# Two value projections by a seven-product block scheme, in a two-layer attention and gated-MLP kernel on one core

## The chip, the core and the metric

The kernel runs on one core of a Trainium2 chip. The metric is the device time of one execution in microseconds; of the kernel before there are three runs, 1532.43, 1533.35 and 1533.71 us, with the median 1533.35. The profile is that of one further execution (1532.7 us, of which 1531.0 us lie between the first and the last instruction). TensorE's granted clock was 1.000 of full speed in it.

Engines are named as in the profile: PE is TensorE's matmul (PEld its weight loads), DVE is VectorE, ACT is ScalarE, POOL is GpSimd, SP is the engine that issues most DMA transfers. "L836" is line 836 of the kernel before.

## The reference, cut to what matters

```python
def _A_ref(x, wqkv, wo):          # B=1, S=2048, D=1024, H=32 heads of Dh=32
    qkv = (x @ wqkv).reshape(B, S, 3, H, Dh).transpose(2, 0, 3, 1, 4)
    q, k, v = qkv[0], qkv[1], qkv[2]
    # each position attends to W=8 positions, 2 apart, backwards
    logits = einsum("bhsd,bhswd->bhsw", q, kg) * Dh ** -0.5   # masked at the start
    attn = softmax(logits)
    o = einsum("bhsw,bhswd->bhsd", attn, vg)
    return o.transpose(0, 2, 1, 3).reshape(B, S, D) @ wo

def _B_ref(x, w1, w3, w2):        # F=3584
    return (silu(x @ w1) * (x @ w3)) @ w2

x = x + _A_ref(layernorm(x), wqkv, wo)      # layer 0, the same weights
x = x + _B_ref(layernorm(x), w1, w3, w2)
x = x + _A_ref(layernorm(x), wqkv, wo)      # layer 1
x = x + _B_ref(layernorm(x), w1, w3, w2)
```

The change concerns the last third of `x @ wqkv`, the values v: a product of a chunk of 512 positions (1024 x 512) with a 1024 x 1024 weight, in layer 1 only.

## The kernel before

The 2048 positions are cut into four chunks of 512. A unit is a layer and a chunk; the eight units' MLP stages follow each other on TensorE, u = 0 to 7. After the MLP stages 1 to 4 come the products q, k and v of the unit three further on, that is of layer 1's chunks 0 to 3. The attention itself runs on VectorE beside the next MLP stages, and its output tiles (matmul with `wo`, "po") are pushed in between MLP groups.

```python
    for u, (l, c) in enumerate(units):
        ...
        q = u + 3
        with_q = 1 <= u and q < len(units)
        b_stage(u, with_q)                       # MLP of the unit
        if with_q:
            for which in range(3):               # q, k, v of unit u + 3
                if which == 2:
                    between(False, True)
                q_part(*units[q], which, [weight("qkv"), weight("qkv")])
                release(2)
```

A part q, k or v is computed plainly: for each of eight output tiles eight matmuls of 128 x 512, a cast out of PSUM by ScalarE (L840), and a store of every two tiles.

```python
    def q_part(l, c, which, ws, then=()):
        ...
            for t in range(t0, t0 + SG):
                ps = bank("ps")
                for kk in range(KT):                                   # KT = 8
                    nc.tensor.matmul(ps[:], lhsT=ws[kk // KH][:, kk % KH, t::KT], rhs=xnT[:, kk, :],
                                     start=(kk == 0), stop=(kk == KT - 1))        # L836
                nc.scalar.copy(sgt[:, t - t0, :], ps[:])                          # L840
            nc.sync.dma_start(qkv_d[l][which][:, t0:t0 + SG, c * CH:(c + 1) * CH], sgt)
```

The MLP stages from u = 2 on compute `x @ w1` and `x @ w3` by a scheme of Strassen's kind: the operands are cut into 2 x 2 blocks, and seven block products (P1 to P7) of sums of blocks stand for eight. The sums of the weights' blocks are made once, stored to device memory (`t_d`) and loaded again for each group as two tiles, "early" (for P1, P5, P6, P2) and "late" (P7, P3, P4). The sums of the activations' blocks are made by VectorE (`norm_sums`, L298; one of them, for P7, overwrites a block of xnT). One product is eight matmuls of 128 x 256.

```python
    def pipeline(key, groups, consume, done, last, fill=None):
        sides = dict(P1=(0, xnT[:, 0:KQ, 0:HT]), P5=(1, sums[:, 0]), P6=(2, sums[:, 1]), P2=(3, xnT[:, KQ:KT, 0:HT]),
                     P7=(0, xnT[:, 0:KQ, HT:CH]), P3=(1, sums[:, 2]), P4=(2, xnT[:, KQ:KT, HT:CH]))
        ...
        def head_part(i, name):
            if name == "P1":
                G["A"] = acc()
                r = run(G, name, G["A"], True)
                G["B"] = acc()
                nc.scalar.copy(G["B"][:], G["A"][:])                 # L1064: P6 and P2 wait for it
            elif name == "P5":
                G["D"] = acc()
                r = run(G, name, G["D"], True)
                nc.scalar.activation(s5, G["D"][:], ACTF.Copy, ...)  # L1069
            elif name == "P6":
                r = run(G, name, G["A"], False, G["tB"])             # adds onto A
                nc.scalar.copy(su, G["A"][:])                        # L1073: P7 waits for it
                nc.vector.tensor_tensor(G["D"][:], G["D"][:], su, op=ALU.add)   # L1076: P3 waits
            elif name == "P2":
                r = run(G, name, G["B"], False, G["tB"])
                consume(G, 0, G["B"][:], r)
            elif name == "P7":
                r = run(G, name, G["A"], False, G["tU"])
                nc.vector.scalar_tensor_tensor(s22, G["A"][:], G["inv"], s5, ...)   # L1088: P4 waits
                consume(G, 3, s22, G["tC"])
            elif name == "P3":
                r = run(G, name, G["D"], False, G["tD"])
                consume(G, 1, G["D"][:], r)
            else:                                                    # P4
                r = run(G, name, G["A"], False, G["tC"])
                consume(G, 2, G["A"][:], r)

        for i in range(n + 1):      # the tail of group i-1 lies between the products of group i
            for name, tail in (("P1", "P7"), ("P5", "P3"), ("P6", "P4"), ("P2", None)):
                if i < n:
                    head_part(i, name)
                if tail and i:
                    head_part(i - 1, tail)
                    if fill and i == n and tail != "P4":
                        fill(int(tail == "P3"))      # in the MLP: first products with w2
```

Before a weight's sums are made its size is measured (squares on ScalarE with an accumulator, one small matmul with ones, a few small VectorE operations) for a power of two that scales it into FP16. Each weight is loaded into one of six tiles; a tile's `release` lets the next load in the fixed sequence start. Background work is placed by the kernel's own estimate of the engines' clocks when it is built: the order within each engine is fixed. Such background work on ScalarE are the normalizations of coming stages (two passes per row block for the moments, L318, and one to apply them, L345), and the exponential of the softmax (L629), which needs another function table than the MLP's Silu.

## Time and profile before

| | before |
|---|---|
| time, median of 3 | 1533.35 us |
| span of the profiled run | 1531.0 us |
| PE busy | 1518.1 us |
| DVE busy | 1201.8 us |
| ACT busy | 884.1 us |
| "ps" matmuls of 128 x 512 (q, k, v; L836) | 1469 recorded, 320.4 us |
| "st" matmuls of 128 x 256 (seven products; L1052) | 4704, 32% of the chain |
| moved by DMA | 439.56 MB, mean 287 GB/s |

A row of the groups gives a line, engine, operation, output and inputs, shape and count, then busy time, the mean of one in ns, and the idle time of the engine ahead of it with what ended it. A matmul's own duration [...] is longer than its distance from the next; the distance is read from the timeline, from start to start. A row of the timeline is a start, a duration, the engine, the line, the operation, and in brackets the idle time ahead with its releaser. The four stages of q, k and v in layer 1 lie at 514.3 to 556.3, 700.7 to 742.6, 885.0 to 926.9 and 1072.7 to 1114.1 us.

### The profile page before, as it was taken

The numbers are of one execution on the slowest core, as the hardware profiler recorded it, in microseconds if no ns is written. First come the engines' busy times: TensorE is split into PE (matmuls) and PEld (weight loads), VectorE is DVE, ScalarE is ACT, GpSimd is POOL, SyncE is SP. The second block draws the span as 40 slices with busy tenths as digits, with TensorE's granted clock in tenths as the row PEclk, the third lists the DMA queues.
The fourth block names the chain that finished last, engine by engine and source line by source line (L and its number), as shares of the span: only waits on it lengthen the run. The fifth ranks groups of instructions, "written<-read, shape, count | busy, mean of one in ns | idle before, by whom it ended". The sixth has DMA issues, their size and how long they took to land.

```text
span 1531.0 us, 25095 instructions
## 1 busy us (share of the span) xinstructions
PE 1518.1 (99%) x9594; PEld 989.5 (65%) x9634; DVE 1201.8 (78%) x2126; ACT 884.1 (58%) x1388; POOL 153.7 (10%) x308
## 2 busy tenths in 40 slices
PE   9999999999999999999999999999999999999999
PEld 7666644444444577575786767766677767686865
DVE  4688998889989898989698958898678986435445
ACT  3885476567665357455565564756557445554643
POOL 1210102121211101001011010100111000000000
PEclk9999999999999999999999999999999999999999
DMA  9777969798997888979779997898969988878885
GB/s 321 202 218 215 253 226 330 272 304 289 306 320 247 280 316 294 347 264 303 263 269 324 346 268 282 280 323 302 323 225 333 338 296 282 306 272 334 318 294 203
DMA packets 261432, 439.56 MB, mean 287 GB/s; under 512 B 73856, under 2 KB 201088, under 8 KB 245056
## 3 DMA queue, kind: packets, MB, share of 16 engines
q1 hardware_dynamic: 248464, 390.90, 76.8%
q0 software_dynamic: 12704, 46.93, 8.6%
q8 instruction: 75, 1.23, 0.3%
q14 instruction: 45, 0.37, 0.1%
q10 hardware_dynamic: 144, 0.13, 0.0%
HBM read 345.90 MB, written 67.90 MB: 270 GB/s over the span
## 4 chain that ended last, share of the span: by engine, by line
PE 97%; ACT 1%; issue 1%; DVE 0%; DMA 0%; SPq 0%; ACTq 0%
PE st L1052 32%; PE ps L836 21%; PE w L1165 16%; PE po L771 7%; PE pg L1279 6%; PE pu L1288 6%; PE acc L1310 6%; PE pq L444 1%; PE L L604 0%; DMA wqkv<-in_A_wqkv_dram 0%; ACT L629 0%; ACT L1227 0%; ACT E L629 0%; ACT sg L1227 0%; DVE x_sb L1150 0%
## 5 line engine op out<-in xcount | busy, mean ns | idle before, releaser
L836 PE MATMUL ps<-xnT,wqkv 128*128 128x512 f16 (+1 forms) x1469 | 320.4, 379 | 0.2
L1052 PEld LDWEIGHTS <-early 128*128 128x128 f16 x2688 | 262.6, 98 | 40.4 <-issue 3.5
L836 PEld LDWEIGHTS <-wqkv 128*128 128x128 bf16 x1472 | 210.6, 144 | 108.1 <-issue 2.2
L1165 PE MATMUL w<-t,hT 128*128 128x512 f16 x1008 | 226.0, 379 | 0.6 <-ACT big L1185 0.5
L1052 PEld LDWEIGHTS <-late 128*128 128x128 f16 x2016 | 197.2, 98 | 30.6 <-issue 2.5
L590 DVE TENSOR_TENSOR tree<-qT,kT 128x2048 bf16<-128x2048 bf16 x128 | 156.3, 1221 | 35.8 <-DMA kT<-qkv_d 18.2
L1052 PE MATMUL st<-xnT,late 128*128 128x256 f16 x1344 | 174.2, 273 | 2.2 <-ACT big L1073 2.2
L510 DVE TENSOR_TENSOR tree<-tree 128x1024 bf16<-128x1024 bf16 x256 | 175.6, 686 | 0.9
L1052 PE MATMUL st<-big,early 128*128 128x256 f16 x1344 | 172.3, 273 | 1.6 <-ACT sg L1227 1.1
L1165 PEld LDWEIGHTS <-hT 128*128 128x128 f16 x1008 | 98.2, 98 | 112.9 <-DVE hT L1136 2.0
L1052 PE MATMUL st<-xnT,early 128*128 128x256 f16 x1344 | 165.7, 273 | 0.0
L665 DVE TENSOR_TENSOR tree<-At,vT 128x2048 bf16<-128x2048 bf16 x128 | 156.2, 1221 | 11.9 <-DMA At<-E 10.7
L1064 ACT COPY st<-st 128x512 f32<-128x512 f32 x84 | 48.3, 575 | 128.1 <-PE st L1052 127.4
L771 PE MATMUL po<-wo,oT 128*128 128x512 bf16 x486 | 110.8, 379 | 1.3
L840 ACT CAST hT<-ps 128x512 bf16<-128x512 f32 x96 | 55.8, 585 | 90.6 <-PE ps L836 88.3
L1288 PE MATMUL pu<-xnT,w3t 128*128 128x512 f16 x448 | 105.8, 379 | 0.0
L1279 PE MATMUL pg<-xnT,w1t 128*128 128x512 f16 x448 | 105.8, 379 | 0.0
L1310 PE MATMUL acc<-w2t,hT 128*128 128x512 bf16 x437 | 97.8, 379 | 0.6
L1076 DVE TENSOR_TENSOR st<-st,big 128x512 f32<-128x512 f32 x84 | 58.4, 695 | 46.9 <-ACT big L1073 46.8
L1227 ACT ACTIVATE sg<-st,down_scale 128x512 bf16<-128x512 f32 x126 | 86.6, 687 | 11.6 <-PE st L1052 11.0
L1052 PE MATMUL st<-big,late 128*128 128x256 f16 x672 | 87.1, 273 | 0.0
L771 PEld LDWEIGHTS <-oT 128*128 128x128 bf16 x512 | 50.1, 98 | 55.7
(167 smaller groups left out, 1916.6 us busy)
## 6 DMA issues: line engine op xcount, KB each, us to landing
early<-t_d SPq DMA_DIRECT2D x84, 1024.0 KB, 6.9
late<-t_d SPq DMA_DIRECT2D x84, 768.0 KB, 6.2
t<-t_d SPq DMA_DIRECT2D x42, 1024.0 KB, 7.3
t<-t_d SPq DMA_DIRECT2D x42, 768.0 KB, 5.3
wqkv<-in_A_wqkv_dram SPq DMA_DIRECT2D x28, 1024.0 KB, 8.1
w1t<-in_B_w_dram SPq DMA_DIRECT2D x14, 1024.0 KB, 7.6
w3t<-in_B_w_dram SPq DMA_DIRECT2D x14, 1024.0 KB, 11.0
t_d<-big POOLq DMA_DIRECT2D x28, 512.0 KB, 6.2
```

What stands on the lines that cost most here:

```text
L510: nc.vector.tensor_tensor(b, b, buf[:, 4:8, :], op=ALU.add)
L590: V.tensor_tensor(pr, qT[:], kT[:, :, k0:k0 + TCH], op=ALU.mult)
L665: V.tensor_tensor(tm.rearrange("p w (a e) -> p w a e", a=4), At[:].rearrange("p a w e -> p w a e"), win, op=ALU.mult)
L771: nc.tensor.matmul(ps[:], lhsT=oT[:, t, j * P:(j + 1) * P], rhs=wo[:, t, hh * 512:(hh + 1) * 512], start=(t == 0), stop=(t == KT - 1))
L836: nc.tensor.matmul(ps[:], lhsT=ws[kk // KH][:, kk % KH, t::KT], rhs=xnT[:, kk, :], start=(kk == 0), stop=(kk == KT - 1))
L1052: nc.tensor.matmul(out[:, a, :], lhsT=w[:, a, blk, k, :], rhs=rhs[:, k, :], start=start and a == 0 and k == 0, stop=k == KQ - 1, skip_grou ...
L1076: nc.vector.tensor_tensor(G["D"][:], G["D"][:], su, op=ALU.add)
L1165: nc.tensor.matmul(out[:], lhsT=lhs[:, k, j * P:(j + 1) * P], rhs=w[:, k, :], start=start and k == 0, stop=k == nq - 1, skip_group_check=True)
L1227: nc.scalar.activation(sg[:], src, ACTF.Silu, scale=inv)
L1279: nc.tensor.matmul(pg[:], lhsT=w1t[:, kk, fi * P:(fi + 1) * P], rhs=xnT[:, kk, :], start=(kk == 0), stop=(kk == KT - 1))
L1288: nc.tensor.matmul(pu[:], lhsT=w3t[:, kk, fi * P:(fi + 1) * P], rhs=xnT[:, kk, :], start=(kk == 0), stop=(kk == KT - 1))
L1310: nc.tensor.matmul(acc[:], lhsT=hT[:, f, j * P:(j + 1) * P], rhs=tiles[hh][f // nq][:, f % nq, :], start=(f == 0), stop=(f == f1 - f0 - 1))
```

## The change

The v part of layer 1's chunks 2 and 3 goes through the seven-product pipeline in place of the plain products. For that, v's weights are measured during the plain v part of layer 1's chunk 0, their block sums are made during chunk 1 (where v is therefore computed first, so that the weight tiles can stay for the sums while q and k follow), stored to device memory and loaded as "early" and "late" tiles in chunks 2 and 3. It is meant to save TensorE one block product in eight. The casts out of PSUM with the scale taken back are ScalarE's in place of the plain casts; one of four blocks comes from VectorE. The sums of the activations' blocks are made for these two chunks as for the MLP.

The core of the diff, with cuts:

```diff
+    size_v = const.tile([P, 8], FP32, name="size_v")
+    down_v = const.tile([P, 1], FP32, name="down_v")
+    up_v = const.tile([P, 1], FP32, name="up_v")
+    blocks += [hT[:, 9:16, :].bitcast(FP16).rearrange("p b (k c) -> p b k c", k=KT // 2)]
+    t_d += [[dram.tile([P, 14, KT // 2, P], FP16, name=f"t_dv_{g}") for g in range(2)]]
...
-            seq += [("qkv", which, h) for which in range(3) for h in range(2)]
+            seq += [("qkv", which, h) for which in ((0, 1, 2), (2, 0, 1), (0, 1))[min(u, 3) - 1] for h in range(2)]
+            if u > 2:
+                seq += [("early", 2, 0), ("early", 2, 1), ("late", 2, 0), ("late", 2, 1)]
...
     def queue_q(q):
         queue_norm(key, units[q][1], range(R))
+        if q > NCH + 1:
+            adds.append([sum_later(key), None])
...
+    def size_of_v(i, w, at):
+        for k in range(KH):
+            yield 1.10, at, lambda: nc.scalar.activation(junk[:, 0:D], w[:, k], ACTF.Square,
+                                                         accum_out=size_v[:, KH * i + k:KH * i + k + 1])
+        if i == 1:
+            total_scale(size_v, up_v, down_v, got_v)
+
+    def sums_of_v(ws, at):
+        ...
+        for g in range(2):
+            for a in range(2):
+                ...
+                for i, (kh, fh) in ((0, (0, 0)), (1, (0, 1)), (3, (1, 0)), (5, (1, 1))):
+                    t = 4 * g + 2 * fh + a
+                    yield 0.65, ..., lambda: nc.scalar.activation(
+                        b[:, i], ws[kh][:, :, t::KT], ACTF.Copy, scale=up_v[:])
+                makes.append([differences(2, g, a, now["act"] + 0.1, slot), None])
...
+    def v_products(l, c):
+        def consume(G, q, src, r):
+            pair, t0 = q % 2, HT * (q // 2)
+            to = stage(G, pair)
+            if q != 3:
+                nc.scalar.activation(to[:, :, t0:t0 + HT], src, ACTF.Copy, scale=down_v[:])
+            ...                      # store when both halves of a pair are there
+        for g in range(2):
+            G = dict(m=2, g=g, inv=down_v[:])
+            G["corner"] = lambda G=G: stage(G, 1)[:, :, HT:CH]
+            groups.append(G)
+        pipeline(key, groups, consume, lambda i: between(False, i == 0), True)    # no fill
+        xnT_free[key] = now["pe"]
...
-            for which in range(3):
-                if which == 2:
-                    between(False, True)
-                q_part(*units[q], which, [weight("qkv"), weight("qkv")])
+            if u == 1:                                   # layer 1, chunk 0
+                ...                                      # q, k, v plain; size_of_v queued in v
+            if u == 2:                                   # layer 1, chunk 1
+                for which in (2, 0, 1):
+                    ...                                  # v, q, k plain; sums_of_v queued in v,
+                    ...                                  # finished after q, then 4 tiles released
+                force(makes, lambda: not any(pending))
+                continue
+            for which in range(2):                       # chunks 2 and 3
+                q_part(*units[q], which, [weight("qkv"), weight("qkv")], (), 1)
                 release(2)
+            v_products(*units[q])
```

## The prediction

> **What bounds the kernel now.** I read the busy shares first, then the chain of waits, then the waits of TensorE alone, and last the timeline at the seams that the change touches. From the page, busy time by engine and the chain that ended last:
>
> ```profile
> PE 1518.1 (99%) x9594; PEld 989.5 (65%) x9634; DVE 1201.8 (78%) x2126; ACT 884.1 (58%) x1388; POOL 153.7 (10%) x308
> ...
> PE 97%; ACT 1%; issue 1%; DVE 0%; DMA 0%; SPq 0%; ACTq 0%
> ```
>
> TensorE is busy for 1518 of 1531 us, and 97% of the chain runs over it. So a matmul taken away is worth its full duration, and a wait put into TensorE's queue costs its full length; no other engine has to be made faster for its own sake. The waits of TensorE, longest first, show how little else there is:
>
> ```profile
> PE st L1052 <- ACT big L1073: 2.2, 1, 2.2
> ...
> PE st L1052 <- ACT sg L1227: 1.1, 1, 1.1
> PE w L1165 <- ACT big L1185: 0.5, 1, 0.5
> PE st L1052 <- ACT st L1064: 0.4, 1, 0.4
> ```
>
> All four lie in layer 1 or the MLP stages before it (in the timeline at 989.8, 669.1, 1066.0 and 1234.1 us), and the chain leads from each to the same thing: the softmax's exponential (E, L629) with its table load stands in ScalarE's queue ahead of a copy that TensorE needs. They depend on where the exponential happens to fall.
>
> TensorE's timeline around layer 1's second chunk (q, k and v are 192 plain products, "ps"; "st" is the seven-product scheme of the MLP):
>
> ```profile
> 700.70 31.24 PE L836 MATMUL ps<-xnT,wqkv 128*128 128x512 f16 x144
> 731.87 0.40 PE L604 MATMUL L<-psm,gather 128*32 128x512 bf16 x4
> 732.20 10.58 PE L836 MATMUL ps<-xnT,wqkv 128*128 128x512 f16 x48
> 742.62 1.04 PE L1052 MATMUL st<-xnT,early 128*128 128x256 f16 x8
> 743.50 1.91 PE L1052 MATMUL st<-big,early 128*128 128x256 f16 x16
> ```
>
> From start to start 144 matmuls take 31.17 us, 0.2165 us each. Eight "st" matmuls, one of the seven products, take 0.873 us from start to start (MLP groups of the same window: 594.44, 595.32, 596.19).
>
> The seam itself, all engines:
>
> ```profile
> 742.82 0.59 ACT L840 CAST hT<-ps 128x512 bf16<-128x512 f32 x1 [1.14 <-PE ps L836]
> 743.50 1.91 PE L1052 MATMUL st<-big,early 128*128 128x256 f16 x16
> 743.75 0.57 ACT L1064 COPY st<-st 128x512 f32<-128x512 f32 x1 [0.34 <-PE st L1052]
> ```
>
> Product P1 runs from 742.62, P5 from 743.50, and P6 adds onto P1's accumulator, so it waits until ScalarE has copied that (L1064). The copy ends at 744.32 and P6's place is 742.62 + 2 x 0.873 = 744.37. The reader should see that the slack is 0.05 us: **anything that stands in ScalarE's queue between the last cast and this copy is a TensorE wait.**
>
> [...] 873/8 is 109.1. So halving the width is nearly free, and seven eighths of the work is seven eighths of the time. [...] 592 without and 711 ns with a scale (L1283, L910), table loads 1283. [...] the mean DMA share in the four q/k/v stages is 0.99, 0.90, 0.91 and 1.04.
>
> **The change part by part.**
>
> *Removed and added on TensorE.* One v part is 64 x 0.2165 = 13.86 us. The new one is 2 groups x 7 products x 0.873 = 12.22 us. Two parts: **-3.28 us**. One small matmul adds up the sizes; such float32 ones have 0.19 us of weight load and 0.21 busy: **+0.15**.
>
> *Head of the new v part, twice.* In the changed program's order ScalarE's queue has, after k's last cast, a normalization (L345 of before, mean 1241 ns), then P1's copy. From the end of k: cast at 0.25, normalization at 0.73 (a cast frees the queue after 0.48, as 703.11 - 702.62 shows), copy 1.97 to 2.54, so P6 starts at 2.59 and not at 1.75: 0.84 us. The second normalization stands ahead of the next copy, but P2 and P1 of the second group lie between, so it should cost nothing. **+1.7.**
>
> *Tail of the new v part, twice.* In the MLP the last three products P7, P3, P4 are interleaved with products of w2; here with nothing. P4 waits for VectorE's sum after P7 (L1088, 748 ns). In VectorE's order attention steps precede that sum: in chunk 2 three (1.14 + 0.34 + 0.61 us without their overlap) stand between P6's sum and P7's. Counting from the end of k: P6's sum of the second group ends at 10.2, these steps at 12.25, P7's sum at 13.0, while P3 ends at 12.2: 0.85. In chunk 3 only two short ones stand there: 0.15. **+1.0.**
>
> *Sizes in chunk 0.* Eight squares of 128x1024 on ScalarE between the casts of v. The trace has the same pair: cast at 713.0, square (L318) 713.47, accumulator read 714.43, next cast 714.71, which is 1.72 us for a product group of 1.73. So it just keeps pace; but the eighth square stands between the last cast and P1's copy of the MLP stage that follows: 0.25 + 0.48 + 1.24 + 0.57, the same 2.54 as above. **+0.85.**
>
> *Sums in chunk 1.* 16 scaled copies (711 ns, 11.4 us of ScalarE) and 16 differences (422 ns, 6.8 us of VectorE) during 27.7 us of v and q, where ScalarE was busy 7.3 of 13.8 and 9.8 of 13.9 us and VectorE full. Two copies and a cast are about 1.9 us against TensorE's 1.73, and six PSUM banks take up the lag. On the path: nothing. But k now comes last, the gather of the next scores stands 8 products (1.73 us) before the seam, and E before the last cast: gather at -2.06, its maximum and difference done near -0.2 (the steps follow at +0.45, +1.18 and end at +1.9), then E, cast, copy. With the table loaded in time nothing is lost, else up to 1.0: **+0.5.**
>
> *What moves.* Later scores shift by up to a stage. The places of E at 979, 1063 and 1228 us, which cost 2.19, 0.47 and 0.41, are gone: they fall in plain products or between w2's copies. One lands within an MLP group of the seventh stage, like that at 669.1 (1.1), one among w2's first products (0.5, my judgement): -3.07 + 1.6 = **-1.5.** The one at 669.1 keeps its neighbours.
>
> *Transfers.* v's weights for a chunk are 3.5 MB for 2 MB, twice, and 3.5 MB are written once. **+0.25**, a judgement: some waits, mostly hidden.
>
> Sum: -3.28 + 0.15 + 1.7 + 1.0 + 0.85 + 0.5 - 1.5 + 0.25 = -0.33 us, so 1533.35 becomes 1533.0. The gain of the eighth product is about eaten by the seams.
>
> **Rivals.** (1) *The clean gain.* The seams cost little, since P6's wait is really only part of what I count or ScalarE gets to the copies earlier: 1530 to 1531. For it: no MLP start in this trace shows a wait. Against it: there the copy has no normalization or square ahead of it. (2) *DMA becomes the bound.* With a share of 0.9 to 1.04 in these stages another 1.5 MB in each of two, and 3.5 MB of stores in chunk 1, at the stage's 270 to 340 GB/s are about 5 and 11 us of transfers; v's and q's weights are also held together in chunk 1, so four loads for the next MLP stage start only with k. If the loads come late, TensorE waits for "early" or "late": 1536 to 1540. For it: the shares. Against it: 13.9 us of k cover those four loads of 3.75 MB (11 us at 340 GB/s), the chunk-3 stage ran at 1.04 without one DMA wait on TensorE, and the new weights are loaded a stage ahead. (3) *Attention comes late.* k last delays the scores of chunk 1 by a part (14 us), and VectorE gets 26 more instructions; if an output tile is then wanted before its values are done, TensorE waits several us. Against it: the output tiles moved back by a group or more in the order too, and VectorE's slices in the last fifth are only 4 to 6 tenths busy. 1535 to 1538.
>
> **Range and chances.** The seams are worked out to perhaps 1.5 us together, the shift of the exponentials to 2, the rivals pull up more than down. 8 in 10: 1529.5 to 1536.5. Two per cent is 30.7 us, ten times anything above: faster 0.003, same 0.99, slower 0.007.
>
> **What would show it.** In the profile after: 128 fewer "ps" matmuls and 224 more "st"; two v parts of about 13.9 and 13.2 us from first P1 to the MLP's P1, each with a wait near 0.84 on the copy of P1 and one on the corner sum; a wait of 0.85 at the start of the MLP stage after layer 1's first chunk; no 2.2 us wait near 989 us. It would be wrong if TensorE waits for a DMA or for oT, if the waits at the v parts are nil (rival 1), or if new waits on E of over 2 us stand elsewhere.

## The result and the profile after

The changed kernel takes 1538.74 us (median of 4 runs, 1538.36 to 1540.13), the kernel before 1532.89 us (4 runs, 1531.49 to 1533.71): a ratio of 1.0041, 95% interval 1.0023 to 1.0058. That is 5.85 us more, where 0.3 us less was predicted, and 2.2 us above the predicted range.

The profiled run spans 1536.7 us, for 1531.0. From the page after, busy time by engine and the chain that ended last:

```profile
PE 1519.5 (99%) x9732; PEld 993.5 (65%) x9732; DVE 1219.0 (79%) x2163; ACT 915.2 (60%) x1428; POOL 158.2 (10%) x316
PE 90%; DVE 5%; DMA 2%; ACT 1%; issue 1%; POOL 0%; SPq 0%; ACTq 0%; DVEq 0%
```

PE is busy 1.4 us *longer* although it has fewer columns to multiply. The chain that ran 97% over PE now runs 5% over DVE and 2% over DMA. ACT has 31.1 us more, of which the prediction had accounted for some 10 us of squares and 11 us of copies; the copies alone take 19.4, as shown below. The waits of PE in the whole kernel after (engine, line, what it waited for; then us in total, times, longest):

```profile
PE st L1092 <- ACT st L1104: 4.0, 5, 1.7
PE L L609 <- DVE psm L519: 3.9, 1, 3.9
...
PE st L1092 <- ACT sg L1303: 1.1, 1, 1.1
PE w L1241 <- ACT big L1261: 0.8, 2, 0.5
...
PE st L1092 <- DVE hT L1128: 0.7, 1, 0.7
...
PE st L1092 <- DVE st L1116: 0.4, 1, 0.4
...
PE st L1092 <- DVE big L303: 0.3, 1, 0.3
```

L1092 is before's L1052 (seven products), L844 was L836 (plain products), L1104 was L1064 (P1's copy), L609 was L604 (gather), L1128 was L1088 (the corner sum: VectorE's sum after P7, which P4 waits for), L303 was L298 (sums of activations). The row that the prediction has nowhere is the second: the gather of the scores, four small matmuls, waits once for 3.9 us on VectorE.

Cutting the spans into stages, from first matmul to first matmul in the timeline of PE, shows where time came and went. Six kernels stand in the table; the last four belong to the experiments below.

| stage (us) | before | after | v only | preparation, neighbours | neighbours | last version |
|---|---|---|---|---|---|---|
| q, k, v of chunk 0 | 42.14 | 42.14 | 42.14 | 42.14 | 42.14 | 42.29 |
| MLP u = 2 | 144.38 | 145.68 | 144.39 | 145.14 | 145.47 | 145.89 |
| q, k, v of chunk 1 | 41.92 | **46.92** | 41.92 | 41.92 | 41.92 | 41.44 |
| MLP u = 3 | 142.35 | 143.85 | 142.52 | 144.51 | 144.18 | 144.79 |
| q, k, v of chunk 2 | 41.92 | 41.91 | 41.90 | 41.92 | 41.91 | 40.46 |
| MLP u = 4 | 145.60 | 145.13 | 143.44 | 147.17 | 144.68 | 142.37 |
| q, k, v of chunk 3 | 41.44 | 41.18 | 40.47 | 41.93 | 41.19 | 41.51 |
| from there to the end | 417.07 | 416.71 | 420.78 | 417.13 | 417.00 | 417.48 |
| sum | 1016.82 | 1023.52 | 1017.56 | 1021.86 | 1018.49 | 1016.23 |

What lies ahead of these stages takes 513 to 515 us in all of them; the profiled run of before has 514.18 there and that of after 513.18, where none of the new work lies, so stages of single profiles compare to about 1 us. A profile is also one execution of several: that of the column "preparation, neighbours" took 1538.54 us, 2.1 more than the median of its runs.

Chunk 1 has the loss: 5.0 of the 6.7 us. PE's timeline at its end, after (start, duration, and in brackets the idle time ahead with its releaser):

```profile
735.75 5.13 PE L844 MATMUL ps<-xnT,wqkv 128*128 128x512 f16 x23
744.78 0.40 PE L609 MATMUL L<-psm,gather 128*32 128x512 bf16 x4 [3.91 <-DVE psm L519]
745.12 3.00 PE L844 MATMUL ps<-xnT,wqkv 128*128 128x512 f16 x8
747.92 1.70 PE L1092 MATMUL st<-xnT,early 128*128 128x256 f16 x8
```

PE stands still for 3.91 us. Then eight plain products take 2.80 us from start to start (1.73 at full rate), and P1 of the MLP 1.54 (to 749.46) for 0.87. The windows of the same stretch (length, busy time of PE, PEld, DVE, ACT and POOL with instructions, then the granted clock, DMA share, GB/s) show why:

```profile
744.00:746.00 2.00, 1.22 (x8) 0.74 (x8) 1.43 (x5) 0.00 (x0) 0.00 (x0) 0.96 1.00 418
746.00:748.00 2.00, 2.00 (x6) 0.73 (x5) 0.66 (x1) 1.28 (x1) 0.00 (x0) 0.50 1.06 433
748.00:750.00 2.00, 2.00 (x14) 1.55 (x13) 1.32 (x2) 1.37 (x4) 0.00 (x0) 0.68 1.06 441
```

After the idle time the clock is 0.50, and some 1.7 us are lost to it. In windows of 0.5 us it is 1.00 to 745.5, then 0.85, six times 0.50, 0.73 from 749.0 and 1.00 from 749.5, which makes half a clock from about 745.85 to 749.27, 3.4 us. The eight plain products count there as busy for 3.00 us (1.95 with a clock that holds, in the run with matmuls in the gap below), so this is also part of why PE's busy time rose.

Behind the gather stands VectorE, and behind VectorE ScalarE. Two of VectorE's rows in chunk 1, after, four differences each:

```profile
712.08 1.68 DVE L932 TENSOR_TENSOR big<-big 128x512 f16<-128x512 f16 x4 [1.71 <-ACT big L963]
...
717.61 1.68 DVE L932 TENSOR_TENSOR hT<-hT 128x512 f16<-128x512 f16 x4 [1.78 <-ACT hT L963]
```

There are two more such waits, 1.56 at 729.26 and 1.33 at 738.09: VectorE, which is busy for 34.1 of the stage's 41.9 us (700.7 to 742.6), loses 6.4 us while it stands ahead of differences whose operands ScalarE hasn't written. The operands are late because of these rows of the groups of that stage (shapes, count, then busy us and mean ns):

```profile
L963 ACT ACTIVATE hT<-wqkv,up_v 128x512 f16<-128x512 bf16 x8 | 9.7, 1279 | 0.0
L963 ACT ACTIVATE big<-wqkv,up_v 128x512 f16<-128x512 bf16 x8 | 9.7, 1260 | 0.0
```

A scaled copy of v's weights takes 1.27 us on the average; the prediction had reckoned 711 ns, from the copies of w1 and w3, which have the same shape and scale. What is different is the source: `ws[kh][:, :, t::KT]`, every eighth column, 16 bytes apart.

### The profile page after: what moved, and what is told of

Read it like the earlier page. It is cut to its first block, busy times and chain, and to the rows that moved or that the text cites. A ratio compares the mean times of both kernels' runs of the same rounds, so it can differ in the third digit from the quotient of the medians.

```text
span 1536.7 us, 25460 instructions
## 1 busy us (share of the span) xinstructions
PE 1519.5 (99%) x9732; PEld 993.5 (65%) x9732; DVE 1219.0 (79%) x2163; ACT 915.2 (60%) x1428; POOL 158.2 (10%) x316
## 4 chain that ended last, share of the span: by engine, by line
PE 90%; DVE 5%; DMA 2%; ACT 1%; issue 1%; POOL 0%; SPq 0%; ACTq 0%; DVEq 0%
PE st L1092 33%; PE ps L844 16%; PE w L1241 14%; PE po L778 7%; PE pg L1355 6%; PE pu L1364 6%; PE acc L1386 6%; DMA xnT<-xn 1%; PE pq L449 1%; DVE tree L595 1%; DVE tree L515 1%; DMA kT<-qkv_d 1%; DVE tree L670 1%; DVE hT L1212 0%; PE L L609 0%
## 5 line engine op out<-in xcount | busy, mean ns | idle before, releaser
L1092 PEld LDWEIGHTS <-early 128*128 128x128 f16 x2816 | 275.6, 98 | 45.5 <-issue 6.9
L844 PE MATMUL ps<-xnT,wqkv 128*128 128x512 f16 (+1 forms) x1344 | 294.2, 380 | 0.0
L844 PEld LDWEIGHTS <-wqkv 128*128 128x128 bf16 x1344 | 192.3, 144 | 99.3 <-issue 3.1
L1092 PEld LDWEIGHTS <-late 128*128 128x128 f16 x2112 | 206.5, 98 | 31.5 <-issue 2.1
L1092 PE MATMUL st<-big,early 128*128 128x256 f16 x1408 | 181.0, 273 | 5.3 <-ACT st L1104 4.0
L1092 PE MATMUL st<-xnT,late 128*128 128x256 f16 x1408 | 182.4, 273 | 0.7 <-DVE hT L1128 0.7
L1092 PE MATMUL st<-xnT,early 128*128 128x256 f16 x1408 | 173.8, 273 | 0.0
L778 PE MATMUL po<-wo,oT 128*128 128x512 bf16 x512 | 115.7, 379 | 0.0
L1104 ACT COPY st<-st 128x512 f32<-128x512 f32 x88 | 50.8, 577 | 103.9 <-PE st L1092 103.4
L1092 PE MATMUL st<-big,late 128*128 128x256 f16 x704 | 91.2, 273 | 0.4 <-DVE st L1116 0.4
L517 DVE TENSOR_TENSOR tree<-tree 128x512 bf16<-128x512 bf16 x192 | 80.3, 418 | 0.0
```

Of the source, the lines that this page charges most:

```text
L517: nc.vector.tensor_tensor(b[:, 0:2, :], b[:, 0:2, :], b[:, 2:4, :], op=ALU.add)
L778: nc.tensor.matmul(ps[:], lhsT=oT[:, t, j * P:(j + 1) * P], rhs=wo[:, t, hh * 512:(hh + 1) * 512], start=(t == 0), stop=(t == KT - 1))
L1092: nc.tensor.matmul(out[:, a, :], lhsT=w[:, a, blk, k, :], rhs=rhs[:, k, :], start=start and a == 0 and k == 0, stop=k == KQ - 1, skip_grou ...
```

## The experiments

**Theory A**: the stride of the copies' source makes them slow; the order of work, fixed when the kernel is built with 0.65 us for a copy, then puts VectorE in front of late operands. **Rival B**: copies and differences are too much work for that stage, whatever a copy takes. **Rival C**: the new transfers delay the inputs of the scores. **Rival D**: the new v parts themselves lose more than they save. (From the v parts alone on, each expectation letters its rivals afresh.) A ratio compares a kernel with runs of the kernel before in the same session (medians 1532.02 to 1533.15 us); the changed kernel's 1538.74 is of another session, so differences from it are good to about 1 us.

### Copies of neighbouring columns, nothing else

```diff
-                        b[:, i], ws[kh][:, :, t::KT], ACTF.Copy, scale=up_v[:])
+                        b[:, i], ws[kh][:, :, t * P:(t + 1) * P], ACTF.Copy, scale=up_v[:])
```

The sums are then of other columns, and v of chunks 2 and 3 is not the reference's; the order, counts and bytes are the changed kernel's.

> The changed kernel, with the same instructions in the same order, but the 16 scaled copies of v's weights read 128 neighbouring columns in place of every eighth (so the sums are of other columns and v of chunks 2 and 3 is not the reference's). Theory A (the every-eighth-column read makes a copy 1.22 us where 0.71 was reckoned; ScalarE falls behind, VectorE waits 6.9 us for it in the differences, the gather of the scores waits 3.9 us for VectorE, and TensorE's clock halves for 3.4 us after that idle time): a pair of copies takes 1.42 us, VectorE's waits ahead of the differences go to under 1.5 us in all, the gather waits for nothing, the clock stays at 1.00: 1533.0 us, some 5.7 us less than the changed kernel. Rival B (16 more copies and 16 differences are simply too much work in that stage, whatever their address pattern): at most 2 us less, 1537 or more. Rival C (the new transfers delay the inputs of the scores): no change, 1538.7.

1534.46 us, ratio 1.0008 [1.0001, 1.0015]: 4.3 us below the changed kernel. Its groups in the same stage:

```profile
L963 ACT ACTIVATE hT<-wqkv,up_v 128x512 f16<-128x512 bf16 x8 | 5.3, 719 | 0.0
L963 ACT ACTIVATE big<-wqkv,up_v 128x512 f16<-128x512 bf16 x8 | 5.3, 718 | 0.0
```

VectorE no longer waits ahead of the differences, the gather doesn't wait, the granted clock of the run is 1.0 (0.999 in the changed kernel's) and chunk 1 takes 41.92 us as before. A wait of 0.83 us comes into sight behind it (the exponential ahead of P1's copy), which had been covered. A holds for most of the loss. B falls, with the same number of copies and differences in the same order, and so does C, with the same transfers.

### The preparation alone

Sizes and sums are made as in the changed kernel, with strided copies, and not used; v of chunks 2 and 3 stays plain.

```diff
-            for which in range(2):
-                q_part(*units[q], which, [weight("qkv"), weight("qkv")], (), 1)
+            for which in range(3):
...
+                q_part(*units[q], which, [weight("qkv"), weight("qkv")])
                 release(2)
-            v_products(*units[q])
```

> Sizes in chunk 0 and sums in chunk 1 as in the changed kernel, with v of chunks 2 and 3 left plain as before (the sums are made and not used). Theory A (the loss is the preparation's, the seven-product parts gain little): chunk 1's stage takes 46.9 us as in the changed kernel, chunk 0 and its MLP stage lose 1.0; the time is 1532.9 + 5.7 + 1.0 = 1539.5 or up to 1 us to either side by where the exponentials fall. Rival D (the seven-product parts lose as well, through their loads): below 1537.5.

1540.95 us, ratio 1.005 [1.0035, 1.0065]. The gather waits 3.90 us and chunk 1 takes 46.51. So the loss is there without any new v part: D falls as the main cause. It is 1.4 us more than expected; 2.65 us of waiting at 937.97 for the sums of the activations (L303, on a transposing transfer) is a wait that the changed kernel has at 0.28 us only.

### The true cost in the estimate

```diff
-                    yield 0.65, max(at, got_v["at"], stored[slot]), lambda: nc.scalar.activation(
+                    yield 1.22, max(at, got_v["at"], stored[slot]), lambda: nc.scalar.activation(
```

The instructions are the same; the order is built in the knowledge that a copy is slow.

> The changed kernel with one number changed: the kernel's own estimate of a scaled copy of v's weights, by which the order on each engine is laid down, is 1.22 us and not 0.65. Theory A: the differences then stand where their inputs are ready, the scores go ahead of them on VectorE, the gather does not wait, the clock stays: 1533 to 1534 us; ScalarE is no less late, so a wait of up to 2 us may remain where the last sums are finished. Rival B (too much work): the wait moves but stays, 1537 or more.

1542.96 us, ratio 1.0067 [1.0049, 1.0084]: worse than the changed kernel, and the expectation missed. The gather doesn't wait any more, but in PE's timeline:

```profile
748.58 5.03 PE L844 MATMUL ps<-xnT,wqkv 128*128 128x512 f16 x16 [7.72 <-ACT hT L848]
```

The copies that found no room earlier are forced out at the end of q, because v's weight tiles must be free for the next loads. There the last four wait 6.26 us (743.62) for a store to leave their buffer, and k's casts, for the first of which PE waits, stand behind them in ScalarE's queue. With the true cost in the estimate the wait is not gone; it stands elsewhere, and is longer.

### Matmuls in the gap

Sixteen matmuls on constants ahead of that gather keep PE busy while it would wait.

```diff
+                if g == 9:
+                    pf = bank("pf")
+                    for i in range(16):
+                        nc.tensor.matmul(pf[:], lhsT=wo[:, 0, 0:P], rhs=wo[:, 0, 0:512], start=True, stop=True)
```

> The changed kernel with 16 matmuls of 128x512 on constant operands (3.5 us, the result is not used) just ahead of the gather that waits 3.9 us in chunk 1. Theory A (of the 5.6 us lost there 3.9 are the wait and 1.7 the half clock that follows the idle time): the wait is filled, the gather starts at the same time, the clock stays at 1.00 after it, and the kernel is 1.7 us faster: 1537.0. Rival (the clock falls for another reason, or the products after the gather are slow for another reason, such as the transfers): no change, 1538.7, with matmuls after the gather still at double distance.

1537.89 us, ratio 1.0035 [1.0023, 1.0046], 0.85 us below the changed kernel, half of what was expected and too little to be sure of by the times alone. The profile says more: the gather waits 0.45, the eight products behind it take 1.79 us for 2.80, P1 0.87 for 1.54. The half clock had cost 1.7 us, but of this 0.82 reappears at once as the exponential's wait ahead of P1's copy (749.81): a slow PE had been waiting for ScalarE without showing it.

### The v parts alone

Chunks 0 and 1 are plain, and nothing of v is measured or summed. The v parts of chunks 2 and 3 load w1's stored sums and scale, so v is not the reference's.

```diff
-            v = t_d[i][n][:, 0:8] if early else t_d[i][n][:, 8:14]
+            v = t_d[i % 2][n][:, 0:8] if early else t_d[i % 2][n][:, 8:14]
...
```

> Only the two seven-product v parts: chunks 0 and 1 are plain, no sizes and no sums of v are made, and the v parts of chunks 2 and 3 load w1's stored sums and w1's scale in place of v's (the values are therefore not the reference's; bytes, products and order of a v part are the changed kernel's). Theory A (the loss of 5 us is all in the preparation, from the copies' true cost): two v parts of 28 products save 3.28 us by count, and their seams hold some 2.1 us of waits, so 1531.7 (1530.5 to 1532.5), below the kernel before. Rival B (the v parts themselves are the loss, through their seams and what they push into the MLPs behind them): 1535 or more. The sum of the prediction's own terms for these parts (minus 3.28, plus 1.7, plus 1.0) says 1532.3.

1532.40 us, ratio 0.9996 [0.9987, 1.0004]. The parts are no loss and nearly no gain, as A has it. In chunk 3 a v part takes 12.36 us (1097.46 to 1109.82), for 13.86 plain: 1.50 us saved. 14 products of 0.873 us are 12.22; the other 0.14 lie ahead of P4. In chunk 2 it takes 13.79, with idle times of 0.55 at its head and 0.69 at its tail. And the MLP of u = 4 is 2.2 us shorter than before while what follows chunk 3 is 3.7 us longer: the wait of 2.19 us at 989.79 is gone, and one of 2.20 stands at 1172.72, behind an exponential with its two table loads (1167.11 to 1170.30 on ScalarE). The windows there, for the v-only kernel:

```profile
1170.00:1172.00 2.00, 0.52 (x5) 0.31 (x4) 1.93 (x4) 1.99 (x4) 0.32 (x1) 1.00 1.19 232
1172.00:1174.00 2.00, 1.28 (x7) 0.95 (x7) 1.95 (x4) 2.00 (x5) 1.95 (x4) 0.73 0.99 280
1174.00:1176.00 2.00, 2.00 (x8) 0.82 (x6) 1.79 (x4) 0.96 (x1) 0.00 (x0) 0.50 0.90 373
```

and for the kernel before around its own 2.19 us:

```profile
988.00:990.00 2.00, 0.21 (x2) 0.19 (x2) 1.97 (x3) 2.00 (x5) 1.24 (x3) 1.00 1.33 176
990.00:992.00 2.00, 2.00 (x15) 1.21 (x13) 1.99 (x4) 2.00 (x3) 1.02 (x2) 1.00 1.07 328
```

The same wait is followed by a clock of 0.50 in one kernel and of 1.00 in the other; what decides between them is not shown, only that the length alone doesn't. Half a clock makes the wait dearer: the product and the eight matmuls with w2 behind the wait take 4.27 us from start to start (1172.72 to 1176.99) for 2.60. One exponential in a bad place is worth 2.2 us or, with the clock, 3.9.

### The differences booked later

```diff
-                makes.append([differences(2, g, a, now["act"] + 0.1, slot), None])
+                makes.append([differences(2, g, a, now["act"] + 2.7, slot), None])
```

> The changed kernel, computing the same, with one constant changed: the differences of v's sums are booked 2.7 us after the copies instead of 0.1, so that VectorE gets the attention's work ahead of them and the gather one group of projection matmuls later. Theory A (VectorE stands in front of differences whose copies are late): the waits ahead of the differences fall by 2 us each at most, the gather's wait of 3.91 us goes below 1 us, the clock keeps its rate, and the time is 1534.5 (1533.5 to 1536). Rival B (ScalarE is simply overbooked in that chunk and something of it ends last whatever the order): over 1537, with the wait at another place of the same chunk.

1539.96 us, ratio 1.0049 [1.0032, 1.0066]. The first half came as A has it: the gather waits 0.19, P1 takes 0.88 us behind it (743.95 to 744.83; 1.54 in the changed kernel), and chunk 1 falls from 46.92 to 43.29 us, of which 1.09 is a wait of P1 for its weights ("early", 743.95). But the MLP behind it rises from 143.85 to 150.26. In PE's timeline:

```profile
770.46 1.86 PE L1092 MATMUL st<-xnT,late 128*128 128x256 f16 x8 [5.32 <-DVE big L1128]
```

and in VectorE's:

```profile
767.79 1.23 DVE L595 TENSOR_TENSOR tree<-qT,kT 128x2048 bf16<-128x2048 bf16 x1 [6.29 <-DMA kT<-qkv_d]
```

VectorE got to the first scores of chunk 1 before the load of their k, stood there for 6.29 us, and the corner sum that PE needs stood behind it. Chunk 1's k is the last part now; its load comes late for scores that are booked early. This is the third rival of the prediction, attention late, in a form that it hadn't named.

### What a stride costs

The sixteen copies read, four by four, neighbouring columns, every second, every fourth and every eighth (sums of other columns; v of chunks 2 and 3 is not the reference's).

> A measurement of the copies by themselves: the first four read 128 neighbouring columns, the second four every second column, then every fourth, then every eighth, with 512 elements each (the sums are of other columns than v's, so the v parts of chunks 2 and 3 do not give the reference's values). If the cost is a matter of the stride being over two bytes: 0.71, 1.27, 1.27, 1.27 us. If it grows with the stride: 0.71, then some 0.8 and 1.0, and 1.27 at the end.

The groups of four of its one run, in this order:

```profile
L963 ACT ACTIVATE big<-wqkv,up_v 128x512 f16<-128x512 bf16 x4 | 2.7, 718 | 0.0
L963 ACT ACTIVATE hT<-wqkv,up_v 128x512 f16<-128x512 bf16 x4 | 2.7, 718 | 0.0
L963 ACT ACTIVATE big<-wqkv,up_v 128x512 f16<-128x512 bf16 x4 | 2.9, 772 | 0.0
L963 ACT ACTIVATE hT<-wqkv,up_v 128x512 f16<-128x512 bf16 x4 | 4.9, 1284 | 0.0
```

Steps of 2 and 4 bytes cost nothing, 8 bytes 8%, 16 bytes 79%. Neither expectation has this form: it is neither any stride nor a steady growth, but an edge between 8 (772 ns) and 16 (1284). What makes the edge is not shown.

### Two columns at a time

Columns t and t + 2 lie 4 bytes apart, a step that cost nothing above (718 ns); the next pair follows 12 bytes on.

```diff
+                t = 4 * g + a
+                for i, kh in ((0, 0), (3, 1)):
+                    yield 1.3, max(at, got_v["at"], stored[slot]), lambda: nc.scalar.activation(
+                        (b[:, 0:2] if kh == 0 else b[:, 3:6:2]).rearrange("p f k c -> p k c f"), ws[kh][:].rearrange(
+                            "p k (c t) -> p k c t", t=KT)[:, :, :, t:t + 3:2], ACTF.Copy, scale=up_v[:])
```

> The changed kernel, computing the same, with the copies of v's weights made two groups of columns at a time: 8 activations of 1024 elements, whose reads step 4 bytes and then 12 (two columns out of every eight), in place of 16 of 512 that step 16 bytes. Theory A1 (the cost goes with each element read out of line): about 2.4 us each, 19 us in all, and the time within 1.5 us of the changed kernel's. Theory A2 (the cost is in how far apart the reads lie, so that a second column near the first is cheap): about 1.6 us each, 13 us in all, VectorE's waits under 0.7 us, and the time 1534.5 or less.

1557.98 us, ratio 1.0163 [1.0148, 1.0179], far from both. The copies:

```profile
L963 ACT ACTIVATE big<-wqkv,up_v 128x1024 f16<-128x1024 bf16 x4 | 19.8, 4960 | 0.0
L963 ACT ACTIVATE hT<-wqkv,up_v 128x1024 f16<-128x1024 bf16 x4 | 19.7, 4915 | 0.0
```

4.8 ns an element, against 2.5 with the plain stride of 16 bytes. The edit gave the read steps of 4 and 12 bytes and made the write jump between two blocks 1 KB (or 2 KB) apart with each element. The author suspected the write, but read and write were changed together, so this run doesn't separate them.

### Neighbouring columns, and v's rows stored where they belong

If a tile holds 128 neighbouring columns, its output rows belong at other rows of v. v in device memory is an array whose flat row is the column of the weight, so one slice does it, with the same number of 1 KB pieces.

```diff
-                        b[:, i], ws[kh][:, :, t::KT], ACTF.Copy, scale=up_v[:])
+                        b[:, i], ws[kh][:, :, t * P:(t + 1) * P], ACTF.Copy, scale=up_v[:])
...
-                nc.sync.dma_start(qkv_d[l][2][:, t:t + SG, c * CH:(c + 1) * CH], to)
+                v_rows = qkv_d[l][2][:].rearrange("i t s -> (i t) s")[t * P:(t + SG) * P]
+                nc.sync.dma_start(v_rows.rearrange("(b p) s -> p b s", p=P)[:, :, c * CH:(c + 1) * CH], to)
```

> The changed kernel, computing the same as the reference: the sums are of neighbouring columns (as in the contiguous run), and the v part writes a tile's 128 rows to the rows of v that neighbouring columns belong to (the same number of transfers, of 1 KB pieces, to other addresses). Theory A (strided copies were the loss): as the contiguous run, 1534.5 (1533.5 to 1535.5). A rival, that the other addresses slow the stores or the loads of v: over 1536, with a wait of the attention behind a load of v.

1534.19 us, ratio 1.0011 [1.0003, 1.0020], as expected, and it computes the whole reference. It takes 4.5 us less than the changed kernel. About 2 us above before remain, while the prediction's sum, which already assumed cheap copies, was 0.3 below.

### Where the last 2 us belong

The preparation alone again, but with copies of neighbouring columns. v of all chunks is plain.

> Sizes and sums of v are made, with copies of neighbouring columns, and not used: v of all chunks is made by plain products, so the result is the reference's. Against the same with strided copies (1540.95) the loss of the copies' stride should go, about 4 to 5 us. Theory A' (preparation done with cheap copies still costs its order of work, about a microsecond in chunk 0 and one behind chunk 1): 1535.5 (1534 to 1536.5), and then the v parts' own gain, 0.5 to 1 us, accounts for the neighbouring-columns kernel's 1534.2. Rival (preparation is free once its copies are cheap, and what is left of the loss is the v parts' seams): 1533 or less.

1536.41 us, ratio 1.0025 [1.0014, 1.0037]. It isn't free: +3.8 us, just within the range of A'. Of the table's stages, the MLPs of u = 2, 3 and 4 take 0.8, 2.2 and 1.6 us more than before. The largest of its waits is in the last of them:

```profile
934.06 2.35 PE L1088 MATMUL st<-big,early 128*128 128x256 f16 x11 [2.45 <-DVE big L303]
```

That is a sum of activations which waits for a transposing transfer of the normalized rows; the sixteen matmuls behind it take 3.21 us from start to start (934.06 to 937.27), for 1.74 in the kernel before (927.77 to 929.51). Preparation +3.8, v parts -0.5 and both together +2.2 don't add up. The profiles show other waits in each of the three: the 2.45 us are not there with both, nor the v-only kernel's 2.20. That each addition changes the order of all later background work would explain it, but no run tests it by itself.

### The squares earlier

Squares of v's weights, which stand ahead of the first P1 copy of the MLP u = 2, are taken in k's part instead of v's.

```diff
-                    if which == 2:
-                        for i in range(2):
-                            lazy.append([size_of_v(i, ws[i], ...), None])
+                    if which == 1:
+                        for i in range(2):
+                            n = used[0] + i
+                            lazy.append([size_of_v(i, w_tiles[n], max(w_at[n], now["pe"] - 5.0)), None])
```

> The kernel with neighbouring columns, and the squares of v's weights taken during k's part of chunk 0 instead of at its end; nothing else is asked for. If the 0.46 and 0.16 us waits at the head of the MLP behind chunk 0 are the squares and nothing more: 1533.5 (1532.5 to 1534.5). If the order of all later work changes with it (the queues are filled by booked times), a wait of over a microsecond appears elsewhere and the time is 1535 or more.

1533.17 us, ratio 1.0004 [0.9995, 1.0013]: no difference from before that this measurement shows. The time is the first expectation's; the wait of over a microsecond is the second's. The waits of 0.46 and 0.16 at the MLP's head are gone, and so are 0.83, 1.69 and 0.69 elsewhere. In their place others came, of which one is large, by the mechanism that the later booking had shown:

```profile
766.03 1.22 DVE L595 TENSOR_TENSOR tree<-qT,kT 128x2048 bf16<-128x2048 bf16 x1 [4.53 <-DMA kT<-qkv_d]
```

PE waits 3.55 us for the corner sum behind it. The profiled execution took 1535.70 us, 2.5 above the median, so not all of this wait need be in the median.

```profile
768.69 1.03 PE L1092 MATMUL st<-xnT,late 128*128 128x256 f16 x8 [3.55 <-DVE big L1128]
```

Here the matmuls keep their rate: the eight products take 0.87 us to the next row (769.56), and the granted clock of the run is 1.0.

### Two attempts that lost

The first adds to the early squares a limit: in the last two tiles ahead of a seven-product part, ScalarE's background work is booked 1.2 us ahead of PE at most, for 2.2, so that P1's copy finds a free engine.

```diff
+                if l == 1 and which == last and t == KT - 2:
+                    gate[0] = 1.2
...
+                gate[0] = 2.2
```

> The one before, with the work on ScalarE around the heads of the seven-product parts moved: the squares of v's weights are taken in k's part of chunk 0, ahead of their head, and in the last two tiles of a part of plain products ScalarE's other work is booked 1.2 us ahead of TensorE at most, for 2.2. The waits of 0.46 (squares), and of 0.55 twice (heads of v, whichever of ScalarE's work stands ahead of P1's copy) should go: 1533.0 (1532 to 1534.5). If they are not of the order of work but of the copy's own length, nothing moves: 1534.5.

1549.01 us, ratio 1.0107 [1.0092, 1.0122]. The two heads of 0.55 us are gone. But the two normalizations that stood there, at 915.62 and 917.85 with neighbouring columns alone, now run at 919.80 and 921.98, and they feed the *next* MLP. The transposing transfer of the second is therefore put behind loads of q, k and weights in the issuing queue, and goes out at 931.55 for 919.33. VectorE, at the sums for that MLP:

```profile
938.08 0.69 DVE L303 TENSOR_TENSOR big<-xnT 128x1024 f16<-128x1024 f16 x1 [9.38 <-DMA xnT<-xn]
```

PE waits 8.17 us there and 5.00 behind chunk 3. What cost 0.55 us at the head was work that had to be early. The second attempt keeps the first and also holds layer 1's exponentials back until plain products or products of w2 run.

```diff
+            while l == 1 and not calm[0]:
+                yield "blocked"
...
```

> The one before, with layer 1's exponentials (each brings two loads of a table on ScalarE, 3.2 us together) kept out of the seven-product parts that need ScalarE within a microsecond: they are put out only while plain products or products of w2 run. If the 2.2 us waits of the kernel before and of the v-only run, and the 0.83 of the contiguous one, are exponentials in the way, they go: 1531.0 (1529.5 to 1533). If the attention behind the later exponentials ends last instead, waits of the projection of the attention's output appear: 1535 or more.

1558.64 us, ratio 1.0165 [1.0148, 1.0182]. The 2.2 us waits are not there, but waits of 3.09, 4.51 and 10.43 us are, the last at 1427.38 for a transfer of normalized rows. What delayed that transfer was not followed. The first attempt's 8.17 and 5.00 us are not in this profile, so its loss is not simply a part of this one, and what holding back costs by itself is not shown. The first attempt missed both of its expectations. In the second the waits of the projection that its rival names are there, 1.02 us at most, but they are not the loss.

### The scores of chunk 1 later

The kernel with early squares, and one half's first score product booked 6.5 us after its load for 2.0, so that VectorE does the corner sum first.

```diff
-            yield 0.0, ready + 2.0, lambda: None
+            yield 0.0, ready + (6.5 if (l, h) == (1, 2) else 2.0), lambda: None
```

> The kernel with early squares, and the first product of q and k of one half of chunk 1 booked 6.5 us after its load for 2.0, so that VectorE doesn't stand before it (4.53 us on the load of k, which the kernel with early squares shows at 766.03) with a corner sum behind it. If that wait is what stood in TensorE's way (3.55 us at 768.69): 1530.0 (1528.5 to 1531.5), below the kernel before for the first time. If the load is late for a reason of its own and the attention ends last behind it, or a wait comes at another place: 1532.5 or more.

1531.45 us (13 runs, 1530.9 to 1533.62) against 1533.15 (17 runs): ratio 0.9991, interval 0.9983 to 1.0000. That is just within the range expected. The corner sum goes ahead at 762.93, the wait of 3.55 us is gone, and PE's waits of over 0.5 us behind the kernel's first stage are:

```profile
PE st L1092 <- ACT big L1113: 1.6, 3, 1.0
...
PE po L778 <- DVE x_sb L783: 1.2, 2, 0.8
PE st L1092 <- ACT sg L1304: 1.1, 1, 1.1
...
PE st L1092 <- ACT st L1104: 0.6, 1, 0.6
```

It computes the whole reference and is the first version with its own seven products for v whose median lies below that of the kernel before. The gain, 1.7 us by the medians, is at the edge of what the interval shows; that it is faster is not shown.

## Why the prediction was wrong, point by point

*What bounds the kernel.* Right: every loss and every gain followed here is an idle time of PE, its clock after one, or matmuls taken away.

*How a wait is measured.* The seams of v in chunk 2, after:

```profile
919.89 1.04 PE L1092 MATMUL st<-xnT,early 128*128 128x256 f16 x8
920.76 1.04 PE L1092 MATMUL st<-big,early 128*128 128x256 f16 x8
922.35 1.03 PE L1092 MATMUL st<-big,early 128*128 128x256 f16 x8 [0.55 <-ACT st L1104]
...
931.08 1.04 PE L1092 MATMUL st<-big,late 128*128 128x256 f16 x8
932.81 1.03 PE L1092 MATMUL st<-xnT,late 128*128 128x256 f16 x8 [0.69 <-DVE hT L1128]
933.68 0.49 PE L1092 MATMUL st<-xnT,early 128*128 128x256 f16 x3
```

The bracket counts idle time from the end of the row before. That row lasts 1.04 us, though without a wait the next starts 0.87 us after it. So what is lost, from start to start, is some 0.17 us more than the bracket says: 0.72 us for 0.55 and 0.86 for 0.69. The sizes below are from start to start, as the prediction's are.

*Removed and added on TensorE, -3.28.* Right: 224 more "st" matmuls, and the lengths of the two new parts are 12.22 us and their waits. The small matmul took 0.14 for 0.15.

*Head of the new v part, +1.7.* The mechanism is right, and the size a little too large: 0.72 twice, 1.4 us. ScalarE's rows are the ones foretold, but a normalization of 1.24 us holds the queue for 1.14 and the cast stood 0.05 earlier:

```profile
920.09 0.58 ACT L848 CAST hT<-ps 128x512 bf16<-128x512 f32 x1 [1.14 <-PE ps L844]
920.57 1.24 ACT L350 ACTIVATE xn<-x_sb,mom 128x1024 f16<-128x1024 bf16 x1
921.71 0.58 ACT L1104 COPY st<-st 128x512 f32<-128x512 f32 x1
```

*Tail, +1.0.* Right: 0.86 and 0.13, for 0.85 and 0.15. The two parts take 13.79 and 13.07 us, where 13.9 and 13.2 were foretold. *Sizes in chunk 0, +0.85.* 0.63 on P1's copy and 0.54 for VectorE behind it (idle 0.46 and 0.37), 1.2 us; the second was not foretold.

*Sums in chunk 1, +0.5.* **This is the step that failed.** "16 scaled copies (711 ns, 11.4 us of ScalarE)" took the duration from copies with the same shape and scale and a contiguous source. Those of v took 1.27 us, 19.4 us together. "Two copies and a cast are about 1.9 us against TensorE's 1.73" was then about 3.0 us. "On the path: nothing" followed from it and fell with it: four waits of VectorE, 6.4 us, the gather's 3.91, half a clock behind it. The stage cost 5.0 us, and P1 behind it 0.67. Neighbouring columns took 4.3 us away by one edit of an index. The rest of the term was sound: with cheap copies the exponential ahead of P1's copy costs 0.99 us from start to start, the "up to 1.0" of the prediction.

*What moves, -1.5.* Also wrong, and hidden behind the larger error. The three exponentials in the way (idle 2.19, 0.47 and 0.41 us; 3.55 from start to start) went, as said. In their place came 0.71, 1.69, 0.49 and 0.36 us, 3.89 from start to start. Only the 0.71 is an exponential: the 1.69 is a normalization that waited for its moments, and the other two are a copy that waited for VectorE. The balance is +0.34. Where background work lands was the worst-known term of the sum, and the range of 2 us given for it was just wide enough; the sign of its middle was wrong.

*Transfers, +0.25.* 0.44 (idle 0.28) at the first sums of the MLP u = 4. In the changed kernel no wait of PE for a weight load shows in layer 1, so the second rival, transfers as the bound, falls.

With the measured sizes the sum is -3.28 + 0.14 + 1.43 + 0.98 + 1.16 + 5.67 + 0.34 + 0.44 = +6.9 us, against 6.7 between the profiles from chunk 0 on and 5.85 by the medians. Of the 7.2 us between this and the prediction's sum, 5.2 are the sums in chunk 1 and 1.8 what moves. Of the rivals the third, attention late, is the nearest, with its 1535 to 1538; but its reason (k comes last) was not what made the changed kernel slow. It became so only in the later booking and the early squares, where the load of k did stop VectorE.

The range was wrong in one way more. It added the uncertainties of the seams and of the exponentials; it had none for a duration carried over from another instruction. Yet the access pattern stood in the diff.

## What to carry to other kernels

A duration taken from a row of the profile held here for the same access pattern, not for the same shape alone (718 ns with a step of 2 bytes, 1284 with 16): ask of every operand how far apart its elements lie, on the read and on the write side. In a kernel whose background work is placed by an estimate, a late producer can show up two engines further on (here ScalarE's copies, then 6.4 us of VectorE, then 3.91 of PE), so follow a new wait back until an instruction is itself longer than booked; and take away a wait by changing the thing that is late, since moving the order around it gave back as much or more in four of six attempts here (the true cost, the later booking and the two that lost). When layout makes a copy slow, look for the index at the far end (here the rows of a store) that lets the copy be contiguous.

## What the runs showed of the hardware that was not expected

- ScalarE's scaled copy of 128 x 512 BF16 elements: 718 ns with steps of 2 and 4 bytes, 772 with 8, 1284 with 16. A pair-wise read with a write that alternates between two blocks 1 or 2 KB apart: 4.9 us for 1024 elements, nearly twice as much for each element again; read or write is not shown.
- Idle times of PE of 2.20 us (v only) and 3.91 us (the changed kernel) were followed by a clock of 0.50, one of 2.19 us (before) by 1.00, and one of 3.55 us (early squares) by matmuls at the full rate, eight in 0.87 us: the length alone did not decide. The two falls cost about 1.7 us each beyond the idle time itself (4.27 for 2.60 us of matmuls behind the 2.20, 2.80 and 1.54 for 1.73 and 0.87 behind the 3.91).
- A wait of PE cost some 0.17 us more, from start to start, than the idle time that the profile shows for it (0.72 for 0.55, 0.86 for 0.69).
